# One tile's x in a full-array matmul and a one-bank buffer, and one batch's sums moved from TensorE to GpSimd

## The chip, the cores and the metric

The kernel runs on one core of one Trainium2 chip. The metric is the device time of the core in microseconds. Ratios here are the mean time of one kernel's fast runs over that of the other's of the same rounds, so they are not quite the ratio of the medians that stand beside them. The trace's span is about 1.8 us shorter than the device time.

## The reference, cut to what matters

```python
# attention with 32 memory slots, per batch and head (B=8, H=8, S=576, D=64, M=32)
a = exp(phi); a = a / a.sum(axis=sequence)          # "the sums": over the sequence
k_m, v_m = a.T @ k, a.T @ v                         # "the pooling"
attn = softmax(q @ k_m.T / 8)
x = attn @ v_m                                      # -> [B, S, 512]
# then a feed-forward block with layer norm and a residual
out = x + relu(layernorm(x) * g @ w_ch1) @ w_ch2    # 512 -> 2048 -> 512
```

Two batches are 1152 rows, which is nine tiles of 128. Tile 4 straddles the two batches; tile 8 is the ninth, and it lies in the second (odd) batch alone.

## The kernel before

Psum is where the matmuls of this kernel write. Tiles of a psum pool "big" have two banks each, three of them; those of "one" have one bank, two of them. `first layer` below means `mm1` (64 matmuls a batch), `second layer` means `mm2` (16 matmuls a tile, psum from "one").

```python
def a_exp(b):
    ...                                   # e = exp(phi) on ScalarE
    if b >= 2:                            # sums over the 9 chunks on GpSimd: six operations,
        ...                               # result split into two bf16 parts "hl"

def a_kv(b):
    ps = big([P, 2, 512], FP32, "kv_ps")
    a_sum(b, ps)                          # b < 2: nine matmuls; else two matmuls with hl
    a_pool(b, ps)                         # 72 matmuls in 64x32 tiles, then k, v and 1/sum out

def x_tiles(pr, ts, stats=True, o_ps=None):   # one or two tiles of x, row-tiled (64 rows each)
    if o_ps is None:
        o_ps = big([P, 2, 512], FP32, "o_ps")
    ...                                   # per tile: 4 matmuls, 8 where it straddles two batches
    x = moe.tile([P, 2, C], FP32, name="x_sb", bufs=4)
    nc.scalar.activation(out=x..., in_=o_ps..., func=AF.Copy)

# for batches b = 1..7; nb = b + 1; the odd ones finish five tiles, t = 4..8
half(0)                                   # first 8 matmuls of the second layer of t[0]
if more and odd:
    o_ps = big(...); kv_ps = big(...)
    a_sum(nb, kv_ps)
    x_tiles(pr, t[0:2], False, o_ps)
    a_pool(nb, kv_ps)
else:
    if more:
        a_kv(nb)
    x_tiles(pr, t[0:2], False)
x_tiles(pr, t[2:4], False)
if odd:
    x_tiles(pr, t[4:5], False)            # the ninth tile: fourth user of three "big" buffers
...
half(1)
```

The softmax here doesn't subtract the row's maximum and nothing guards it: scores larger than these inputs give would overflow.

## Time and profile before

| | before |
|---|---|
| device time, median of the first 3 runs | 250.44 us (250.23 to 250.91) |
| TensorE matmul busy | 95% of the span |
| chain that ended last | TensorE 77%, transfers 17% |
| first transposes of batch 1's q, second half | 47.1 us |
| first layer of batch 1 starts | 53.8 us |

The chain of waits is the view to read: up to 45 us it is transfers, after that TensorE to the end. The prediction shows its lines. Batch 7 in the chain in order of time (start, length, what), where there is no pooling left to do:

```profile
226.95 1.67 PE ch_ps L481 x7
228.62 0.79 PE o_ps L442 x24
229.41 3.99 PE ch_ps L481 x18
```

and GpSimd's first load for batch 4 in the timeline, which follows directly on the last of batch 3's sums:

```profile
80.72 0.43 POOL L201 TENSOR_TENSOR hl<-es,hl 128x128 bf16<-128x128 f32 x1
81.21 0.79 POOL L84 DMA_DIRECT2D kv_bf<-in_k_dram  x1
```

### The profile page before, as it was taken

Reading aid. Unit: us, or ns where it says so; the run is one execution under the profiler, and the core shown is the slowest. Engines: PE = TensorE matmul, PEld = TensorE weight load, DVE = VectorE, ACT = ScalarE, POOL = GpSimd, SP = SyncE. Lnnn points to the kernel's source line nnn. Section 1 sums busy time; section 2 is a strip of 40 time slices with the busy share of each in tenths; the row PEclk is TensorE's granted clock in tenths of the full one; section 3 lists DMA queues with packets and bytes.
Section 4 is the critical chain, followed back from the end, with each engine's and each line's share of the span. In section 5 each row is a group of like instructions: output and inputs, shape, how many; then the busy total and the mean of one; then the engine's idle time right before and its main releaser. Section 6 shows DMA issues by size and latency. Waiting matters only on the chain.

```text
span 248.8 us, 5860 instructions
## 1 busy us (share of the span) xinstructions
PE 236.5 (95%) x2460; PEld 132.2 (53%) x2491; DVE 156.0 (63%) x304; ACT 130.0 (52%) x219; POOL 60.7 (24%) x100
## 2 busy tenths in 40 slices
PE   7979899999999999999999999999999999999994
PEld 2544554457544665467544674466544764476442
DVE  3247663685577656687569637685679538783641
ACT  3164572587554465837472656655580755465310
POOL 8643241022325402090206202170205001000000
PEclk9999999999999999999999999999999999999999
DMA  7999999998499799919965997429983301203133
GB/s 150 190 202 206 207 256 213 286 223 148 119 174 236 116 216 245 179 20 194 262 122 117 146 242 168 104 37 221 211 167 68 73 14 43 45 12 75 42 84 84
DMA packets 42451, 36.82 MB, mean 148 GB/s; under 512 B 17461, under 2 KB 37689, under 8 KB 42425
## 3 DMA queue, kind: packets, MB, share of 16 engines
q0 software_dynamic: 17776, 19.53, 46.9%
q1 hardware_dynamic: 24488, 16.79, 28.4%
q8 instruction: 19, 0.31, 0.5%
q10 hardware_dynamic: 160, 0.13, 0.2%
q14 instruction: 8, 0.06, 0.1%
HBM read 41.42 MB, written 9.44 MB: 204 GB/s over the span
## 4 chain that ended last, share of the span: by engine, by line
PE 77%; DMA 17%; issue 2%; ACT 2%; POOL 1%; DVE 0%; POOLq 0%
PE ch_ps L481 45%; PE h_ps L411 22%; DMA q_bf<-in_q_dram 8%; DMA w1r<-in_moe_w_ch_dram 6%; DMA kv_bf<-in_k_dram 3%; PE w1b_ps L390 3%; PE o_ps L442 2%; PE last_ps L493 1%; ACT x_sb L448 1%; PE sc_ps L328 1%; PE den_ps L359 1%; PE kv_ps L210 1%; POOL q_bf L92 1%; PE qT_ps L310 0%; ACT qT L313 0%
## 5 line engine op out<-in xcount | busy, mean ns | idle before, releaser
L481 PE MATMUL ch_ps<-w2b,rT 128*128 128x512 bf16 x531 | 123.0, 379 | 2.3 <-issue 1.6
L481 PEld LDWEIGHTS <-rT 128*128 128x128 bf16 x560 | 52.1, 98 | 63.5 <-issue 6.5
L411 PE MATMUL h_ps<-Eh,w1b 128*128 128x288 bf16 x512 | 66.4, 285 | 1.3 <-ACT rT L417 1.0
L417 ACT ACTIVATE rT<-h_ps 128x576 bf16<-128x576 f32 x88 | 52.2, 648 | 26.8 <-PE h_ps L411 26.8
L411 PEld LDWEIGHTS <-w1b 128*128 128x128 bf16 x512 | 49.5, 97 | 18.1 <-issue 2.4
L394 DVE SCALAR_TENSOR_TENSOR w1b<-m_sb,rsum,w1b_ps 128x512 bf16<-128x512 f32 (+1 forms) x66 | 44.2, 726 | 8.5 <-PE w1b_ps L390 6.1
L419 DVE TENSOR_SCALAR rT<-h_ps 128x576 bf16<-128x576 f32 x40 | 30.3, 758 | 25.2 <-PE h_ps L411 24.6
L505 DVE SCALAR_TENSOR_TENSOR x_sb<-ch_ps,rstd,x_sb 128x512 f32<-128x512 f32 x35 | 26.1, 745 | 9.5 <-PE ch_ps L481 6.4
L461 DVE BATCH_NORM_STATS2 bst<-x_sb 128x6 f32<-128x512 f32 x36 | 24.3, 676 | 6.4 <-ACT x_sb L448 6.4
L448 ACT ACTIVATE x_sb<-o_ps 128x1024 f32<-128x1024 f32 (+1 forms) x20 | 17.8, 939 | 16.1 <-PE o_ps L442 16.0
L287 POOL TENSOR_TENSOR vb<-v,vmask 128x256 bf16<-128x256 bf16 x12 | 7.8, 664 | 60.9 <-DVE rs L237 60.9
L194 POOL TENSOR_TENSOR es<-e_sb 128x512 f32<-128x512 bf16 x6 | 6.9, 1156 | 62.2 <-ACT e_sb L187 62.2
L467 ACT ACTIVATE rstd<-mv,eps_sb 128x2 f32<-128x2 f32 (+1 forms) x20 | 5.9, 297 | 30.8 <-DVE mv L462 30.6
L333 ACT ACTIVATE E_sb<-sc_ps,rs 128x640 bf16<-128x640 f32 x16 | 11.8, 790 | 12.8 <-PE sc_ps L328 12.8
L375 DVE SCALAR_TENSOR_TENSOR Eh<-E_sb,rs,rden 128x576 bf16<-128x576 bf16 x16 | 12.4, 814 | 8.8 <-ACT rden L374 8.8
L179 PE MATMUL w_ps<-fill 128*128 128x512 f32 (+1 forms) x16 | 10.5, 774 | 1.6 <-DVE fill L119 1.6
L227 DVE CAST k<-kv_ps 128x256 bf16<-128x256 f32 x7 | 3.0, 425 | 13.8 <-PE kv_ps L210 13.8
L390 PE MATMUL w1b_ps<-w1r,kvT 64*32 64x512 bf16 (+1 forms) x264 | 10.9, 374 | 0.1
L187 ACT ACTIVATE e_sb<-phi_st 128x1152 bf16<-128x1152 f32 x8 | 9.2, 1151 | 2.7 <-DMA phi_st<-in_phi_dram 2.7
L374 ACT ACTIVATE rden<-rden 128x576 f32<-128x576 f32 x16 | 10.0, 672 | 0.1
L92 POOL DMA_DIRECT2D q_bf<-in_q_dram x10 | 7.6, 757 | 4.6 <-DMA w2b<-in_moe_w_ch_dram 1.8
L210 PE MATMUL kv_ps<-kv_bf,e_sb 64*32 64x128 bf16 (+1 forms) x648 | 7.4, 215 | 0.7 <-DMA kv_bf<-in_v_dram 0.4
(76 smaller groups left out, 150.9 us busy)
## 6 DMA issues: line engine op xcount, KB each, us to landing
out_dram<-x_sb SPq DMA_DIRECT2D x70, 128.0 KB, 2.9
kv_bf<-in_k_dram POOLq DMA_DIRECT2D x7, 576.0 KB, 6.1
kv_bf<-in_v_dram POOLq DMA_DIRECT2D x7, 576.0 KB, 9.5
phi_st<-in_phi_dram SPq DMA_DIRECT2D x6, 576.0 KB, 4.9
q_bf<-in_q_dram POOLq DMA_DIRECT2D x6, 576.0 KB, 13.6
w2b<-in_moe_w_ch_dram POOLq DMA_DIRECT2D x4, 512.0 KB, 17.8
w1r<-in_moe_w_ch_dram POOLq DMA_DIRECT2D x3, 512.0 KB, 14.2
q_bf<-in_q_dram POOLq DMA_DIRECT2D x4, 288.0 KB, 12.6
```

The costliest lines, as they stand in the source:

```text
L179: nc.tensor.matmul(w_ps[:, 0:N], fill[:, 0:P], fill[:, 0:N], start=True, stop=True)
L333: nc.scalar.activation(out=E_[:, g].rearrange("p (a x) -> p a x", a=2), in_=sc[:, :, 0:HP], func=AF.Exp, scale=s["rs"][:, g:g + 1])
L375: nc.vector.scalar_tensor_tensor(out=Eh[:, g, :], in0=s["E"][:, g, 0:S], scalar=s["rs"][:, g:g + 1], in1=rd[:, g].rearrange("p a x -> p (a ...
L390: nc.tensor.matmul(ps[32 * j:32 * (j + 1), g, 0:N], s["kvT"][r:r + 64, 2, 32 * j:32 * (j + 1)], w1r[r:r + 64, j, fs], start=True, stop=Tru ...
L394: nc.vector.scalar_tensor_tensor(out=s["w1b"][:, g, fs], in0=m_sb[:, fs], scalar=s["rsum"][:, g:g + 1], in1=ps[:, g, 0:N], op0=ALU.mult, o ...
L411: nc.tensor.matmul(h_ps[:, half, 0:HS], s["w1b"][:, g, P * j:P * (j + 1)], s["Eh"][:, g, HS * half:HS * (half + 1)], start=(g == 0), stop= ...
L417: nc.scalar.activation(out=dst, in_=h_ps[:, :, 0:HS], func=AF.Relu)
L419: nc.vector.tensor_scalar(out=dst, in0=h_ps[:, :, 0:HS], scalar1=0.0, scalar2=None, op0=ALU.max)
L448: nc.scalar.activation(out=x[:, 0:n].rearrange("p i (u y) -> p i u y", u=2), in_=o_ps.rearrange("p u (i y) -> p i u y", i=2)[:, 0:n], func ...
L461: nc.vector.bn_stats(out=stt, in_=x)
L481: nc.tensor.matmul(ch_ps, rT[:, j, P * t:P * (t + 1)], w2b[:, j, :], start=(j == 0), stop=(j == JC - 1))
L505: nc.vector.scalar_tensor_tensor(out=x, in0=ch_ps, scalar=rstd, in1=x, op0=ALU.mult, op1=ALU.add)
```

## The change

The ninth tile's x lies in one batch, so it can use the whole array: two matmuls with all 128 rows, into one bank of the small pool, rather than four with 64 rows into a large buffer. Its copy on ScalarE comes between those of the two pairs. The pooling comes ahead of all x, as in even batches. Apart from that, the sums of batch 1 move to GpSimd and behind that batch's pooling.

```diff
@@ a_exp
-        if b >= 2:
+        if b >= 1:
@@ a_kv, a_sum, a_pool
-        a_sum(b, ps)
-        a_pool(b, ps)
+        if b == 1:
+            a_pool(b, ps, lambda: a_sum(b, ps))     # called after the 72 matmuls
+        else:
+            a_sum(b, ps)
+            a_pool(b, ps)
     def a_sum(b, ps):
-        if b < 2:
+        if b < 1:
             kv_sum(b, ps)
@@ x_tiles: ahead of its copy
+        if mid is not None:
+            mid()
@@ new
+    def x_one(pr, t):
+        o_ps = one([P, C], FP32, "o1_ps")
+        ...
+        for g in range(2):
+            nc.tensor.matmul(
+                o_ps.rearrange("p (j e d) -> p j e d", e=2, d=D)[:, :, g, :],
+                s["Eh"][:, g, a:a + P], s["vb"][:, g].rearrange("p j d -> p (j d)"),
+                start=True, stop=True)
+        x = moe.tile([P, 2, C], FP32, name="x_sb", bufs=4)
+        nc.scalar.activation(out=x[:, 0], in_=o_ps, func=AF.Copy)
@@ batch loop
-        if more and odd:
-            ...                                     # first pair ahead of the pooling
-        else:
-            if more:
-                a_kv(nb)
-            x_tiles(pr, t[0:2], False)
-        x_tiles(pr, t[2:4], False)
-        if odd:
-            x_tiles(pr, t[4:5], False)
+        if more:
+            a_kv(nb)
+        x_tiles(pr, t[0:2], False)
+        x_tiles(pr, t[2:4], False, (lambda: x_one(pr, t[4])) if odd else None)
@@ start of batch 1
+    load(2)
     a_exp(1)
 ...
-    load(2)
     a_exp(2)
```

More of the change, by code (lines that the diff above doesn't have):

```diff
@@ L252, in a_sum, with a_pool @@
                                  start=(i == 0), stop=(i == 1))
-    def a_pool(b, ps):
+    def a_pool(b, ps, late_sum=None):
         kv_mm(b, ps, slice(0, 2))
+        if late_sum is not None:
+            late_sum()
         k_out(b, ps, b < 2)
@@ L422, with x_tiles @@
     xs = {}
-    def x_tiles(pr, ts, stats=True, o_ps=None):
+    def x_tiles(pr, ts, stats=True, mid=None):
         n = len(ts)
-        if o_ps is None:
-            o_ps = big([P, 2, 512], FP32, "o_ps")
+        o_ps = big([P, 2, 512], FP32, "o_ps")
         for i, t in enumerate(ts):
@@ L456, in x_tiles @@
                 x_stats(pr, t)
+    def x_one(pr, t):
+        o_ps = one([P, C], FP32, "o1_ps")
+        b = 2 * pr + P * t // S
+        a = P * t % S
+        s = st8[b]
+        for g in range(2):
[5 more added lines that the diff above has]
+        nc.scalar.activation(out=x[:, 0], in_=o_ps, func=AF.Copy)
+        mv = moe.tile([P, 2, 2], FP32, name="mv", bufs=4)
+        xs[(pr, t)] = (x[:, 0, :], mv, 0, 1)
     def x_stats(pr, t):
@@ L618 @@
         half(0)
-        if more and odd:
-            o_ps = big([P, 2, 512], FP32, "o_ps")
-            kv_ps = big([P, 2, 512], FP32, "kv_ps")
-            a_sum(nb, kv_ps)
-            x_tiles(pr, t[0:2], False, o_ps)
-            a_pool(nb, kv_ps)
-        else:
-            if more:
-                a_kv(nb)
-            x_tiles(pr, t[0:2], False)
-        x_tiles(pr, t[2:4], False)
-        if odd:
-            x_tiles(pr, t[4:5], False)
+        if more:
+            a_kv(nb)
+        x_tiles(pr, t[0:2], False)
+        x_tiles(pr, t[2:4], False, (lambda: x_one(pr, t[4])) if odd else None)
         if nb + 1 < B:
```

## The prediction

> **What bounds the kernel now.** I read four views: the busy shares, the chain of waits that ended last, the chain in order of time, and the timeline around the places that the change touches.
>
> The shares and the head of the chain first:
>
> ```profile
> PE 236.5 (95%) x2460; PEld 132.2 (53%) x2491; DVE 156.0 (63%) x304; ACT 130.0 (52%) x219; POOL 60.7 (24%) x100
> ...
> PE 77%; DMA 17%; issue 2%; ACT 2%; POOL 1%; DVE 0%; POOLq 0%
> ```
>
> The second line is the one to use: 77% of the span hangs on TensorE, 17% on transfers, and only 2% (about 5 us) on ScalarE. The chain in order of time shows where each lies. All the DMA is before 45.2 us (k, then a part of w1, then q of batch 1); after that it is TensorE to the end. So TensorE time that goes after 45.2 us is gained in full, and TensorE time that goes before is waited away on the transfer.
>
> Now the place where the ninth tile's x is made, batches 1, 3 and 5 (batch 3 looks the same as batch 1):
>
> ```profile
> 62.30 1.67 PE ch_ps L481 x7
> 63.97 0.03 PE kv_ps L251 x2
> 64.00 0.47 PE o_ps L442 x12
> 64.47 0.02 issue
> 64.50 1.03 ACT x_sb L448
> 65.53 0.04 issue
> 65.57 0.29 PE o_ps L442 x4
> 65.86 0.16 issue
> 66.02 1.67 PE ch_ps L481 x7
> ```
>
> Columns: start, length, what. Tempting reading: TensorE waits 1.03 us for a copy. The timeline corrects it:
>
> ```profile
> 64.38 0.80 PE L210 MATMUL kv_ps<-kv_bf,e_sb 64*32 64x128 bf16 x72
> 64.50 2.57 ACT L448 ACTIVATE x_sb<-o_ps 128x1024 f32<-128x1024 f32 x3 [2.03 <-PE o_ps L442]
> 65.12 0.74 PE L442 MATMUL o_ps<-vb,Eh 64*128 64x128 bf16 x12
> 65.57 0.11 PEld L442 LDWEIGHTS <-Eh 64*128 64x128 bf16 x3 [0.18 <-issue]
> ```
>
> During the copy TensorE does the 72 matmuls of the next batch's pooling and the second pair's x. Only the ninth tile's last group of four has to wait for the first pair's psum buffer (three large buffers: first pair, pooling, second pair; the ninth tile is the fourth user). The weight load before it sat idle for 0.18 us. So the wait is worth some 0.2 us a time, three times, not 1 us.
>
> From the last second-layer matmul's end to the next one's start it takes 66.02 - 63.97 = 2.05 us in batch 1, and 2.05 and 2.06 us in batches 3 and 5. The even batches, with pooling and four tiles, show the same stretch without a copy in it:
>
> ```profile
> 91.75 1.67 PE ch_ps L481 x7
> 93.43 0.03 PE kv_ps L251 x2
> 93.46 0.73 PE kv_ps L210 x72
> 94.19 0.55 PE o_ps L442 x16
> 94.74 0.16 issue
> 94.90 1.67 PE ch_ps L481 x7
> ```
>
> That is my yardstick: 0.034 us for each tiled x matmul, and 0.16 us of nothing when TensorE goes from tiled to full matmuls.
>
> Last, the sums of batch 1:
>
> ```profile
> 42.37 0.37 PE L218 MATMUL kv_ps<-ones,e_sb 128*128 128x2 bf16 x9
> 42.95 0.66 PEld L210 LDWEIGHTS <-e_sb 64*32 64x32 bf16 x72 [0.30 <-DMA kv_bf<-in_v_dram]
> 42.95 0.80 PE L210 MATMUL kv_ps<-kv_bf,e_sb 64*32 64x128 bf16 x72 [0.22 <-DMA kv_bf<-in_v_dram]
> ...
> 45.19 0.56 PEld L310 LDWEIGHTS <-q_bf 128*128 128x128 bf16 x10 [0.48 <-DMA q_bf<-in_q_dram]
> ```
>
> The nine sum matmuls stand before a wait for v and, a little later, one for q. Both are ended by transfers.
>
> **What the Trainium skill says.** "TensorEngine Tiling (Array Packing)", Key Properties: a change of tiling mode drains TensorE. The trace agrees: 0.16 us of idle where tiled x matmuls give way to full ones. "PSUM — Partial Sum Buffer", rule 1 of the four PSUM rules: one matmul's output fits in one bank of 512 fp32. That is why a full-array version of one tile (512 values a partition) fits the small buffer, while the row-tiled one, which runs two row tiles at once, spreads over two banks. "TensorE: Matmul & The Clock Gate", Back-to-back issue gap: 262 cycles for N=256 at the warm clock, or 0.109 us as an estimate from that page; the first layer agrees in this trace: 64 matmuls of 288 columns in 7.96 us are 0.124 us each, hence 0.11 us at 256. "GPSIMD Engine Reference", section 3.1: some 2.6 cycles an element for a two-input add. At 512 elements and 1.2 GHz that is 1.11 us as an estimate; the trace has 1.156 us.
>
> **The change part by part.**
>
> Ninth tile, batches 1, 3, 5. Removed: four row-tiled matmuls (4 x 0.034 = 0.14 us) and the wait of about 0.2 us. Added: two full matmuls of 256 columns, 2 x 0.11 = 0.22 us. The drain of 0.16 us is only moved, from ahead of the second layer to ahead of the two. Moved: the pooling now comes ahead of all x, as it does in even batches. New stretch: sums 0.03, pooling 0.73, first pair 0.47 (12 matmuls, eight of them for the tile that straddles two batches), second pair 8 x 0.034 = 0.27, drain 0.16, ninth tile 0.22, together 1.88 us against 2.05. Gain 0.17 us a time. Taking the x of b=7, whose 24 tiled matmuls last 0.79 us, as measure, the two pairs cost 0.79 - 0.14 = 0.65 us and the sum is 1.79: gain 0.26. I take 0.2, times three: 0.6 us.
>
> Ninth tile, batch 7. No pooling there and no buffer wait before: 24 matmuls in 0.79 us straight into the second layer. After: 0.65 + 0.22 plus perhaps a drain of 0.16, so 0.87 to 1.03. Loss 0.1 to 0.25, taken as 0.15 us.
>
> Buffers: the ninth tile takes the second of the two small psum buffers. I looked at which wait the next second-layer tile then carries: it is on ScalarE (the ninth tile's copy), not on the output of the tile before, so it takes the same buffer. The copy comes second on ScalarE (1.02 for the first pair, 0.60 for it), and ends about 1.7 us after the first pair is ready, while that tile starts some 2.7 us after. No stall. The copies and statistics come about 0.7 us later than before against an earlier TensorE, but the outputs that need them free a buffer only two tiles on, about 2.5 us of slack.
>
> Sums of batch 1. Removed: nine loads and matmuls, 42.16 to 42.74 us. All of it lies before the wait for v, so TensorE arrives earlier and waits longer: gain 0. Added on the path: two matmuls after the pooling, 0.03 us if the sums are there. Are they? The exponential starts at 38.60 and takes 1.15 us, to 39.75. GpSimd has issued its last load by 38.4. Batch 3's six operations ran from 77.28 to 81.15, 3.87 us; started 0.08 us after the exponential they end here at 43.70. The pooling ends at 42.95 + 0.73 = 43.68. That is a dead heat; with the wait's latency I expect the next second-layer matmul 0.05 to 0.3 us later than the 43.91 of now. Until q lands at 45.15 there are about 0.3 us of slack (0.30 us idle before the transposes), so most of it is swallowed. Cost taken as 0.1 us. The loads of batch 2 are moved in the text only: GpSimd's order has them in the same place, ahead of the new sums, with the same waits.
>
> Sum: -0.6 + 0.15 + 0.1 = -0.35 us.
>
> **The rivals.** (a) The whole 1.03 us of the copy in the chain is gained three times, 3.1 us less: about 247.3. Against it: the 72 pooling matmuls run within that time, and they must run somewhere. (b) GpSimd's sums come late, held by the shared port or slower than in batch 3 (the second one took 0.94 instead of 0.73 us beside a VectorE operation), and batch 1's kv evacuation, transposes and w1b all shift: 0.5 to 1 us more, about 251. For it: nothing after 45.2 us recovers lost time. Against it: VectorE runs one operation between 39.8 and 43.7, the output addition at 40.85. (c) The two full matmuls cost a second drain or an exposed weight load each: 0.2 us in four batches, so the gain is nil, 250.5. (d) An earlier TensorE in odd batches reaches a wait on the scores or on the first-layer weights sooner, and gives the gain back; the vector work for the next batch ends 6 us ahead of its use there, so I give it little.
>
> **Range and chances.** 250.44 - 0.35 = 250.09; I say 250.1. Range 249.4 to 250.8: the upper end holds (c) and half of (b), the lower a gain of 0.3 us a time with nothing lost elsewhere. The runs of before spread over 0.7 us by themselves. Two per cent would be 5 us, and no part of the change touches that much: same 0.98, faster 0.012, slower 0.008.
>
> **What would show it right or wrong.** In the changed profile: the stretch between second-layer matmuls in batches 1, 3, 5 at about 1.85 us, no ScalarE copy in the chain there; the stretch of batch 7 at 0.9 to 1.0 us; two x matmuls of 128 rows with about 0.11 us between them, after a single gap of 0.16; the first transposes of batch 1's q still at 45.2 us and still released by the transfer; GpSimd's sums ending at about 43.7 us. I am wrong if a wait for the sums on GpSimd stands in the chain, if the second-layer tile after the ninth tile's x waits on ScalarE, or if the q transfer itself lands at another time.

## The result, and the profile after

| | before | after |
|---|---|---|
| device time, median (4 runs each) | 250.61 us (250.23 to 250.91) | 250.62 us (250.24 to 250.69) |
| ratio, 95% interval | | 1.0 (0.9986 to 1.0014) |
| span of the profiled execution | 248.8 us | 248.8 us |

The spans agree to a tenth. The page's shares and chain for the changed kernel:

```profile
PE 239.4 (96%) x2476; PEld 132.2 (53%) x2476; DVE 156.5 (63%) x304; ACT 129.8 (52%) x219; POOL 64.2 (26%) x106
...
PE 79%; DMA 17%; POOL 1%; issue 1%; ACT 1%; DVE 0%; POOLq 0%
```

TensorE seems to do 2.9 us more work. It does not. The weight loads went from 2491 to 2476, which is right: nine sum matmuls fewer and two more, sixteen tiled x matmuls fewer and eight full ones more, in all 15 fewer. The matmuls went from 2460 to 2476 although they too are 15 fewer: the trace of the kernel before lacks 31 matmul records, this one lacks none. The changed kernel profiled again (e2) lacks 31 records too and reads 236.7 us, so the 2.9 us are the records. Busy time of a trace with missing records can't be compared, and it has a second effect, shown next.

The stretch around the x of batch 1, in the chain in order of time:

```profile
62.72 1.73 PE ch_ps L503 x8
64.44 0.03 PE kv_ps L254 x2
64.47 0.73 PE kv_ps L210 x72
65.20 0.68 PE o_ps L446 x20
65.88 0.33 PE o_ps L471 x2
66.21 1.73 PE ch_ps L503 x8
```

No copy in the chain, and TensorE goes without a break. Compare the groups of second-layer matmuls: `x8` in 1.73 us here, "0.16 issue" and then `x7` in 1.67 us in the kernel before. The eighth matmul of the group was run there too; its record is missing, and the gap is where it was. So the 0.16 us that I took for a drain was not all drain: where full matmuls follow full ones, the same missing record leaves a gap of 0.05 us (`62.24 0.05 issue` in the kernel before, then `x7` in 1.67 us). The rest is the drain. It is seen here as 1.83 instead of 1.73 us for eight matmuls after tiled ones (even batch, next fence), and as 0.33 us for two matmuls that stream in 0.22: 0.10 to 0.11 us.

So ends, not starts, must be compared. From the end of half(0) to the end of half(1): before 67.69 - 63.97 = 3.72 us, after 67.93 - 64.44 = 3.49 us. That is 0.23 us gained, in each of batches 1, 3 and 5. (67.69 and 67.93 are the starts of the transposes that follow in each chain.)

Batch 7 loses, as foreseen:

```profile
226.84 1.73 PE ch_ps L503 x8
228.57 0.68 PE o_ps L446 x20
229.25 0.32 PE o_ps L471 x2
229.57 12.09 PE ch_ps L503 x56
```

1.00 us of x instead of 0.79, but 0.10 of the difference is the drain that the next group pays in the kernel before. From batch 7's first layer to the start of the last matmuls it is 22.77 instead of 22.66 us: 0.11 lost.

Three times 0.23 less 0.11 is a gain of 0.6 us. Where did it go? Two places. The first is an even batch, number 2:

```profile
93.67 0.03 PE kv_ps L254 x2
93.70 0.73 PE kv_ps L210 x72
94.43 0.55 PE o_ps L446 x16
94.98 1.83 PE ch_ps L503 x8
...
96.98 1.73 PE ch_ps L503 x8
98.71 0.10 issue
98.81 0.47 PE sc_ps L333 x16
```

TensorE stops for 0.10 us ahead of the scores of batch 3 and then does them in 0.47 us rather than 0.40. In the kernel before there was no such stop.

The second is the opening. Timeline of the changed kernel:

```profile
43.29 0.43 POOL L201 TENSOR_TENSOR hl<-es,hl 128x128 bf16<-128x128 f32 x1
43.32 0.80 PE L210 MATMUL kv_ps<-kv_bf,e_sb 64*32 64x128 bf16 x72 [0.75 <-DMA kv_bf<-in_v_dram]
44.05 0.20 PE L254 MATMUL kv_ps<-ones,hl 128*128 128x2 bf16 x2
...
45.38 0.56 PEld L315 LDWEIGHTS <-q_bf 128*128 128x128 bf16 x10 [0.23 <-DMA q_bf<-in_q_dram]
...
47.58 0.56 PEld L315 LDWEIGHTS <-q_bf 128*128 128x128 bf16 x10 [0.65 <-DMA q_bf<-in_q_dram]
```

GpSimd's sums end at 43.72 us, and their two matmuls start at 44.05, straight behind the pooling: no wait. But v came at 43.3 and not 42.95 us, and the second half of q at 47.5 and not 47.1 us, and batch 1's first layer started at 54.28 and not 53.81 us. That 0.47 us, with the 0.18 us in batch 2, eats the gain. The question for the experiments is whether either belongs to the change.

For the steps from here on I use one table: starts of the first layer of batches 1 to 7 and of the last matmuls, read from the chain in order of time. The first column is when batch 1 starts; "tail" is from there to the start of the last matmuls; "1 to 2" is counted from the group after batch 1's first wait, which is 1.3 us after the start in all of them. Where nothing stops TensorE these steps repeat to 0.03 us between traces of the same code, while times of whole runs scatter by 0.5 us and more: the kernel before, over its 43 runs, went from 249.84 to 252.98 us, mean 250.79.

| trace | batch 1 | tail | 1 to 2 | 2 to 3 | 3 to 4 | 4 to 5 | 5 to 6 | 6 to 7 | 7 to last |
|---|---|---|---|---|---|---|---|---|---|
| before | 53.81 | 187.79 | 28.63 | 25.43 | 29.46 | 25.43 | 29.45 | 25.43 | 22.66 |
| after | 54.28 | 187.38 | 28.40 | 25.61 | 29.22 | 25.43 | 29.22 | 25.43 | 22.77 |
| e1 before again | 54.86 | 187.80 | 28.63 | 25.43 | 29.46 | 25.43 | 29.46 | 25.42 | 22.67 |
| e2 after again | 54.13 | 187.49 | 28.40 | 25.71 | 29.22 | 25.43 | 29.23 | 25.43 | 22.77 |
| e3 ninth tile only | 55.28 | 187.21 | 28.41 | 25.43 | 29.22 | 25.43 | 29.23 | 25.43 | 22.77 |
| e4 sums only | 54.20 | 187.99 | 28.63 | 25.62 | 29.46 | 25.43 | 29.45 | 25.43 | 22.67 |
| e5 order only | 54.68 | 187.69 | 28.60 | 25.42 | 29.43 | 25.43 | 29.42 | 25.42 | 22.67 |
| e6 ninth tile, b7 tiled | 54.24 | 187.26 | 28.40 | 25.59 | 29.22 | 25.43 | 29.22 | 25.43 | 22.67 |
| e7 sums slowed | 56.98 | 187.23 | 28.40 | 25.46 | 29.22 | 25.43 | 29.22 | 25.42 | 22.78 |
| e9 transpose early | 54.00 | 187.20 | 28.40 | 25.43 | 29.23 | 25.43 | 29.22 | 25.42 | 22.78 |
| e10 best | 53.77 | 187.10 | 28.40 | 25.43 | 29.23 | 25.43 | 29.22 | 25.42 | 22.67 |

(e8 and e11 are not in it: their chain leaves TensorE within batch 1 to 2; their tails are 187.45 and 187.94.)

### The profile page after: what moved, and what is told of

It reads as the page before. It is cut to its first block, busy times and chain, and to the rows that moved or that the text cites. A ratio compares the mean times of both kernels' runs of the same rounds, so it can differ in the third digit from the quotient of the medians.

```text
span 248.8 us, 5868 instructions
## 1 busy us (share of the span) xinstructions
PE 239.4 (96%) x2476; PEld 132.2 (53%) x2476; DVE 156.5 (63%) x304; ACT 129.8 (52%) x219; POOL 64.2 (26%) x106
## 4 chain that ended last, share of the span: by engine, by line
PE 79%; DMA 17%; POOL 1%; issue 1%; ACT 1%; DVE 0%; POOLq 0%
PE ch_ps L503 45%; PE h_ps L416 22%; DMA q_bf<-in_q_dram 8%; DMA w2b<-in_moe_w_ch_dram 6%; DMA kv_bf<-in_v_dram 4%; PE w1b_ps L395 3%; PE kv_ps L210 2%; PE o_ps L446 2%; PE last_ps L515 1%; PE sc_ps L333 1%; PE den_ps L364 1%; POOL q_bf L92 1%; PE o_ps L471 1%; POOL kv_bf L84 1%; ACT qT L318 0%
## 5 line engine op out<-in xcount | busy, mean ns | idle before, releaser
L503 PE MATMUL ch_ps<-w2b,rT 128*128 128x512 bf16 x560 | 128.3, 379 | 0.0
L527 DVE SCALAR_TENSOR_TENSOR x_sb<-ch_ps,rstd,x_sb 128x512 f32<-128x512 f32 x35 | 26.1, 746 | 9.7 <-PE ch_ps L503 7.8
L454 ACT ACTIVATE x_sb<-o_ps 128x1024 f32<-128x1024 f32 x16 | 16.0, 1026 | 18.2 <-PE o_ps L446 18.2
L194 POOL TENSOR_TENSOR es<-e_sb 128x512 f32<-128x512 bf16 x7 | 8.1, 1154 | 59.2 <-ACT e_sb L187 59.2
```

The costliest lines, as they stand in the source:

```text
L454: nc.scalar.activation(out=x[:, 0:n].rearrange("p i (u y) -> p i u y", u=2), in_=o_ps.rearrange("p u (i y) -> p i u y", i=2)[:, 0:n], func ...
L503: nc.tensor.matmul(ch_ps, rT[:, j, P * t:P * (t + 1)], w2b[:, j, :], start=(j == 0), stop=(j == JC - 1))
L527: nc.vector.scalar_tensor_tensor(out=x, in0=ch_ps, scalar=rstd, in1=x, op0=ALU.mult, op1=ALU.add)
```

## The experiments

**Theory A**: the change gains some 0.5 us after the opening, and the opening's 0.47 us is chance. **Theory B**: the sums on GpSimd, or the moved load, delay the opening.

### e1 and e2: both kernels again

No edit.

> The kernel before, unchanged, for the spread of its transfers and of its time. Theory A (the change gains some 0.5 us after 45 us, and the one profile of it had its q land 0.4 us later by chance): ratio 1.000 within 0.001, and the first transposes of q's second half start anywhere between 46.9 and 47.8 us; from the first h_ps matmul after the wait at about 55 us to the end it takes 193.7 us whatever the start. Theory B (the change itself delays the transfers): here the second half of q's transposes stay near 47.1 us.

> The changed kernel, unchanged. Theory A: q's second half again lands somewhere between 46.9 and 47.8 us, with no tie to the change; the part after the batch 1 start is 193.2 us; the ratio over many rounds falls to 0.998 (0.5 us of 250). Theory B: q's second half lands late again, at 47.5 us or more, and the ratio is 1.000.

| | median | ratio, 95% interval | batch 1 starts | tail |
|---|---|---|---|---|
| e1 before again | 250.76 us | 1.0008 (0.9975 to 1.0041) | 54.86 | 187.80 |
| e2 after again | 250.28 us | 0.9983 (0.9949 to 1.0017) | 54.13 | 187.49 |

The kernel before started batch 1 a full 1.05 us later than in its own first trace, and later than either trace of the changed kernel. In e2 q's second half was taken up at 47.2 us, where theory B expected 47.5 or more. So the opening scatters by more than the 0.47 us in question, whatever the kernel, and theory B has lost its reason; an effect smaller than this scatter is not excluded. In one of the traces the granted clock offers a cause. Columns of the windows view: stretch, its length, busy time and count of TensorE, weight loads, VectorE, ScalarE, GpSimd, then granted clock, transfers' share, GB/s. The kernel before, first trace, and after it e1:

```profile
16.00:20.00 4.00, 3.50 (x34) 1.97 (x34) 3.26 (x8) 2.74 (x6) 1.50 (x2) 1.00 1.27 205
```

```profile
16.00:20.00 4.00, 3.00 (x19) 1.61 (x18) 1.80 (x6) 2.57 (x5) 1.50 (x2) 0.65 1.28 204
```

Here TensorE ran at 0.65 of its clock for four microseconds of the opening and did 19 matmuls where it did 34; transfers moved the same. That it is the cause is not shown: in the same stretch e2 had a clock of 0.63 and e6 of 0.57, and they started batch 1 at 54.13 and 54.24 us, while e5 had 1.00 and started at 54.68. In the changed kernel's first trace the clock was 1.00, and there it was the transfers that came 0.3 us later: GpSimd issued the second half of q at 28.74 us, 28.41 in the kernel before, at a point where both programs had run the same instructions.

e2 also shows the dead heat between the sums and the pooling, this time lost. The sums on GpSimd started 0.6 us later here (40.49 us, 39.86 in the changed kernel's first trace). The granted clock was 0.63 from 16 to 20 us in this trace too, which may be why; that is argued, not shown:

```profile
43.93 0.43 POOL L201 TENSOR_TENSOR hl<-es,hl 128x128 bf16<-128x128 f32 x1
43.98 0.18 PE L254 MATMUL kv_ps<-ones,hl 128*128 128x2 bf16 x1
44.41 0.18 PE L254 MATMUL kv_ps<-ones,hl 128*128 128x2 bf16 x1 [0.25 <-POOL hl L201]
```

### e3 and e4: each part alone

e3 is the changed kernel with the sums of batch 1 as before; e4 is the kernel before with only the sums moved.

```diff
# e3, against the changed kernel (and load(2) back to its place)
-        if b >= 1:        # a_exp
+        if b >= 2:
-        if b < 1:         # a_sum
+        if b < 2:
-        if b == 1:        # a_kv: sums first again in every batch
-            a_pool(b, ps, lambda: a_sum(b, ps))
# e4, against the kernel before: the same lines the other way round
```

> Only the ninth tile's part; the sums of batch 1 on TensorE as before. Theory A: 193.2 us from batch 1's first layer to the end, ratio 0.998. Theory B (the sums on GpSimd delay the start): ratio 0.998 here too but 1.000 for the whole change, q landing near 47.1 us.

> Only the sums of batch 1 on GpSimd, after the pooling; the ninth tile as before. Theory A: ratio 1.000, the nine matmuls lay before a wait for v; 193.7 us from batch 1's first layer to the end. Theory B: ratio 1.001 to 1.002, the start of batch 1's first layer 0.4 us later than in the kernel before.

| | median | ratio, 95% interval | tail | step 2 to 3 |
|---|---|---|---|---|
| e3 ninth tile only | 250.30 us | 0.9988 (0.9953 to 1.0023) | 187.21 | 25.43 |
| e4 sums only | 251.20 us | 1.0028 (0.9990 to 1.0065) | 187.99 | 25.62 |

The steps add up. The ninth tile alone takes 0.58 us off the tail (three times 0.23, less 0.11) and leaves batch 2 alone. The sums alone add 0.20 us, all of it in batch 2, some 55 us after the sums were made. My expectation for e4's tail, the same as before, was wrong. Both times are inconclusive.

### e5: the order alone

```diff
# against the kernel before
-        if more and odd:
-            ...                                # first pair, then pooling
-        else:
-            if more:
-                a_kv(nb)
-            x_tiles(pr, t[0:2], False)
+        if more:
+            a_kv(nb)
+        x_tiles(pr, t[0:2], False)
```

> Only the order of the change: the pooling ahead of all x, and the ninth tile still row-tiled, in the large buffers. If the small buffer is what makes the order affordable: the ninth tile's four matmuls now wait for the first pair's copy, which starts only when the pooling and the first pair are done; the stretch from the end of one second-layer half to the end of the next grows from 3.7 to about 4.4 us in batches 1, 3, 5, a loss of 0.7 us a time or 2 us, ratio 1.008. If the order itself is what gains: ratio below 1.

Measured: median 250.72 us, ratio 0.9991 (0.9952 to 1.0030), tail 187.69 us. Expected was a loss of 2 us; there is none, and a gain of 0.03 us a time. The timeline:

```profile
65.53 1.17 PE L442 MATMUL o_ps<-vb,Eh 64*64 64x128 bf16 x24
...
66.09 2.43 ACT L448 ACTIVATE x_sb<-o_ps 128x1024 f32<-128x1024 f32 x3 [2.76 <-PE o_ps L442]
...
66.40 0.12 PEld L442 LDWEIGHTS <-Eh 64*128 64x128 bf16 x4 [0.30 <-DVE rs L237]
```

With the pooling first, the large buffer that comes free first is the pooling's, emptied by VectorE's three short operations, and not the first pair's, which ScalarE still copies. The pool gives the ninth tile that one. It waits 0.30 us for the reciprocal, not 0.7 us for the copy. So the order without the small buffer gains next to nothing: of the 0.23 us, 0.20 is the small buffer with its full matmuls.

### e6: the ninth tile of batch 7 as before

```diff
# against e3
-        x_tiles(pr, t[2:4], False, (lambda: x_one(pr, t[4])) if odd else None)
+        x_tiles(pr, t[2:4], False, (lambda: x_one(pr, t[4])) if odd and more else None)
+        if odd and last:
+            x_tiles(pr, t[4:5], False)
```

> Candidate for the best: only the ninth tile's part, and in batch 7, where nothing had to wait, the ninth tile row-tiled as before; sums of batch 1 on TensorE. From batch 1's first first-layer matmul to the end of the last one of the kernel: 191.46 us in the kernel before, 3 x 0.23 less is 190.77, and 0.1 less than with the ninth tile of batch 7 as full matmuls. Ratio 0.997. If the full matmuls cost nothing in batch 7, 190.9 as with the ninth tile's part alone.

Measured: median 250.23 us, ratio 0.9985 (0.9938 to 1.0031); batch 7 takes 22.67 us again, 0.10 less than with full matmuls. The tail was 187.26 and not 187.1 us, because batch 2 took 25.59 us here, with no sums on GpSimd at all. So those sums are not what the stop in batch 2 needs.

### e7: the sums slowed

```diff
# against the changed kernel
-            nc.gpsimd.tensor_tensor(out=a4, in0=ev[:, 0:4], in1=ev[:, 4:8], op=ALU.add)
+            for _ in range(3 if b == 1 else 1):
+                nc.gpsimd.tensor_tensor(out=a4, in0=ev[:, 0:4], in1=ev[:, 4:8], op=ALU.add)
```

> The changed kernel with GpSimd's first add of batch 1 done three times: the sums end 2.4 us later, about 46.2 us. If the sums are at the edge of the path, TensorE waits for them after the pooling for some 2 us, and the first layer of batch 1 starts 1.5 to 2 us later than with the sums as changed: ratio 1.006 to 1.008. If the wait for q hides them: 1.000.

Measured: median 253.73 us, ratio 1.0111 (1.0071 to 1.0151). Batch 1 starts at 56.98 us, 2.7 us later than in the changed kernel's first trace.

```profile
45.18 0.29 POOL L201 CAST hl<-es 128x128 bf16<-128x128 f32 x1
45.52 0.10 PEld L255 LDWEIGHTS <-hl 128*128 128x128 bf16 x1 [2.08 <-POOL hl L201]
...
46.03 0.18 PE L255 MATMUL kv_ps<-ones,hl 128*128 128x2 bf16 x1 [0.32 <-POOL hl L202]
```

TensorE waits 1.95 and then 0.32 us for GpSimd, and nothing later gives it back: the wait for q is used up. The loss is larger than expected. So the sums stand right at the edge of the path: 2.4 us of delay cost all of it, and as changed they have no slack to speak of.

### e8: six tiny fills in the place of the six operations

```diff
# against e3 (with load(2) ahead of a_exp(1), as in the changed kernel)
+    padt = consts.tile([P, 2], FP32, name="padt")
     load(2)
+    for _ in range(6):
+        nc.gpsimd.memset(padt, 0.0)
     a_exp(1)
```

> Only the ninth tile's part, with six tiny fills on GpSimd in the place where the six operations of batch 1's sums stand. All three profiles with those sums show a wait of 0.43 us ahead of GpSimd's load of batch 4's k, and a step from batch 2's first layer to batch 3's of 25.61 us; none of the three without them does (25.43). If it is the number of GpSimd's instructions that does it: the wait and 25.61 here too. If it is what those operations do or what waits on them: no wait, and 25.43.

Measured: median 250.35 us, ratio 0.9973 (0.9936 to 1.0011). GpSimd's load of batch 4's k in the timeline, the changed kernel first, then e8:

```profile
80.95 0.43 POOL L201 TENSOR_TENSOR hl<-es,hl 128x128 bf16<-128x128 f32 x1
81.81 0.79 POOL L84 DMA_DIRECT2D kv_bf<-in_k_dram  x1 [0.43 <-issue]
```

```profile
80.15 0.43 POOL L201 TENSOR_TENSOR hl<-es,hl 128x128 bf16<-128x128 f32 x1
81.00 0.79 POOL L84 DMA_DIRECT2D kv_bf<-in_k_dram  x1 [0.43 <-issue]
```

The wait of 0.43 us is there with six fills that feed nothing. All six traces with just six more GpSimd instructions (after, e2, e4, e8, e9, e11) have it; none of those with no more (before, e1, e3, e5, e6, e10) has it, nor e7 with eight more. It goes with where the instruction stands in GpSimd's stream. Why is not shown, but the kept traces hold a hint: of the queue that the page calls "instruction", q14, all six have one packet in the DMA view between 79 and 86 us, and none of the other seven has any. So GpSimd may have waited for its next instructions to be fetched.

The step from 1 to 3 took 54.08 us here, 0.24 more than e3's 53.84. And here the chain itself runs through the stop, and names it:

```profile
84.38 13.57 DMA qT<-q_bf
97.95 0.14 issue
98.08 0.47 PE sc_ps L330 x16
```

The scores of batch 3 wait for the transpose of q by DMA, which landed 13.6 us after its issue. In the kernel before it took 13.2 us and landed at 84.94 + 13.2 = 98.1 us, 0.26 us ahead of the scores at 98.40. Less than half of that is slack. In the seven traces in which the scores are held up (after, e2, e4, e6, e7, e8, e11) they start 0.14 us after the landing, in those in which they are not and the transpose has its old place (before, e1, e3, e5) 0.24 to 0.27 us after it. So there was some 0.12 us of slack, and what the transpose takes beyond it is the stop: 0.30 us longer gives 0.18 us (after), 0.85 us longer gives 0.73 us (e11, from batch 1 to 3). The chain of e2 names another releaser, a VectorE output (`98.01 0.76 DVE x_sb L527`). That is a coincidence: in the kernel before this output ends at 98.7 us, when the scores have already started.

The transposes of the traces without the stop took 13.2 us (before, e1, e3, e5) or 13.4 (e7, held up by 0.03 us), with it 13.5 to 14.1 us (after, e2, e4, e6, e8, e11). All five traces with GpSimd's late load and the transpose in its old place (after, e2, e4, e8, e11) belong to the second group; but e6, with no late load, does too. So the late load may lengthen the transpose, by coming into its time, and is not its only cause.

### e9: the transpose of batch 3's q issued earlier

In batch 1 it stands behind the outputs of tile 7 in the sync queue, and so waits for that tile's second layer, though its data landed 4 us earlier.

```diff
# against the changed kernel
-            mm2_out(pr, t[3])
             if b == 1:
                 a_qT(nb + 1, 0)
+            mm2_out(pr, t[3])
```

> The changed kernel, with the transpose of batch 3's q issued ahead of the outputs of the tile before instead of behind them. In the three profiles with batch 1's sums on GpSimd the step from batch 2's first layer to batch 3's is 25.61 us, not 25.43, and I put that down to this transpose landing 13.5 us after its issue, just too late for the scores. If so: the transpose lands about 95 us, the step is 25.43 again, and from batch 1's first layer to the start of the last matmuls it takes 187.2 us, not 187.4 to 187.5. If the delay has another cause, the step stays at 25.61.

Measured: median 250.37 us, ratio 0.9994 (0.9970 to 1.0018). The transpose is issued at 80.2 us and lands 10.0 us later, the step from batch 2 to 3 is 25.43 us, and the tail 187.20 us, although GpSimd's late load is there (0.41 us). The starts in the chain:

```profile
83.69 7.96 PE h_ps L416 x64
109.12 7.96 PE h_ps L416 x64
138.35 7.96 PE h_ps L416 x64
```

That settles the stop in batch 2: it is the transpose's landing, and an earlier issue takes it away. The time of this call's runs does not show it; three of the six had a mean clock of 0.993 or less over the whole run, and where in the run is not on record.

### e10: the parts that gain, together

e6 and the early transpose.

> Candidate for the best: the ninth tile as full matmuls in batches 1, 3 and 5 only, sums of batch 1 on TensorE, the transpose of batch 3's q issued early. From batch 1's first layer to the start of the last matmuls 187.80 - 3 x 0.235 = 187.1 us, with steps of 29.70, 25.43, 29.22, 25.43, 29.22, 25.43 and 22.67. Ratio 0.997, which the scatter of the opening may hide.

Measured: median 250.37 us, before 250.80 us in the same rounds, ratio 0.9981 (0.9964 to 0.9998), tail 187.10 us with every step as expected. It is the only version here whose interval lies below 1, and by 0.0002; among eleven runs that would be weak evidence alone, and it is the steps that carry it. The gain is 0.2%.

### e11: batch 1's sums ahead of its pooling

```diff
# against the changed kernel
-        if b == 1:
-            a_pool(b, ps, lambda: a_sum(b, ps))
-        else:
-            a_sum(b, ps)
-            a_pool(b, ps)
+        a_sum(b, ps)
+        a_pool(b, ps)
```

> The changed kernel with batch 1's sums ahead of its pooling, as in all later batches. GpSimd's sums end at 43.7 us and the pooling's v lands at 43.0 to 43.3: TensorE now waits for GpSimd 0.4 to 0.7 us longer, and the pooling ends as much later, at 44.5 instead of 44.0. Of that the wait for q's second half swallows most: the first layer of batch 1 starts 0 to 0.5 us later, ratio 0.998 to 1.001.

Measured: median 251.45 us, ratio 1.0015 (0.9991 to 1.0039). TensorE waits 0.71 and 0.33 us for the two parts of the sums, the pooling starts at 44.36 us, and batch 1's first layer at 54.78 us, 0.5 us later than in the changed kernel's first trace. The tail of 187.94 us has the longest of the transposes in it, 14.1 us. So where GpSimd makes these sums, the place behind the pooling is the better one; it hides about 0.7 us of the wait. The wait is in the trace; that the later start comes from it is argued, as the opening scatters by as much.

## Why the prediction was right or wrong

The time was right: 250.1 predicted, 250.62 measured, inside 249.4 to 250.8, and no difference over 2% as forecast. The ten runs of the changed kernel have a mean of 250.42 us, the 43 runs of the kernel before 250.79: the difference of 0.37 us is close to the 0.35 predicted, but it is smaller than the scatter of single runs and shown by the steps of the traces, not by the times. That the sum came out is partly luck. By the steps 0.70 us were gained in batches 1, 3 and 5, 0.11 lost in batch 7 and 0.18 to 0.28 in batch 2. The last was not foreseen; it fell where the prediction had a gain 0.1 us too small and 0.1 us set aside for the opening.

- **What bounds it, and the rival of 1.03 us a time**: right. The copy left the chain and 0.23 us a time came back (28.63 to 28.40, 29.46 to 29.22 us), because the pooling ran under the copy.
- **Gain of 0.2 us a time, 0.6 in all**: right in sum (0.23 and 0.7), but terms were mis-read. Of the "0.16 us of nothing" taken for a drain some 0.05 us is the missing record of one matmul; the drain is 0.10 us (1.83 less 1.73). A tiled x matmul takes 0.028 us and not 0.034 (in batch 7, 24 took 0.79 us before and 20 take 0.68 now: 0.11 for four). So four tiled matmuls gave way to two full ones that cost 0.11 us more, and what the wait and the old order cost was, as an estimate, 0.23 + 0.11 = 0.34 us rather than 0.2.
- **Loss in batch 7, 0.15 us**: 0.11 measured, just the dearer matmuls. Part of a drain was counted in the 0.15, but the drain is paid in the kernel before too.
- **The next second-layer tile takes the ninth tile's small buffer and doesn't wait**: right; no ScalarE copy in the changed chain. That the order alone would cost 0.7 us a time (e5's expectation) was wrong: another large buffer comes free first.
- **Sums of batch 1: nine matmuls gained nothing, a dead heat with the pooling, 0.1 us**: the dead heat is right, to 43.72 against 44.05 us in one trace and 0.25 us of wait in another. e7 shows how near it is. Whether 0.1 us is lost in the opening can't be told: batch 1 starts anywhere from 53.48 us (e8) to 55.28 us (e3) in traces without the sums on GpSimd, from 54.00 to 54.28 in those with them behind the pooling and not slowed.
- **"An earlier TensorE in odd batches reaches a wait on the scores ... so I give it little"**: this is the step that failed. There was such a wait, in batch 2, an even one where I had not looked, with some 0.12 us to spare, and it took back 0.18 to 0.28 us of the 0.6. I looked at VectorE's work for the next batch and not at the transpose by DMA that the same scores need. It was not TensorE's earlier arrival that used up the slack: the transpose is issued 1.20 us after batch 2's first layer starts in both kernels, so it moves along, and e3 kept the slack. It was a transpose 0.3 us longer. Why it took longer stays open.
- **"The loads of batch 2 are moved in the text only"**: right for those loads. That six more GpSimd instructions would hold up a load of batch 4 by 0.43 us was not foreseen.
- **q at another time** was named as what would make me wrong. It landed 0.4 us later in the changed trace, before which the programs had not differed. In e1 batch 1 of the unchanged kernel starts later still, although q's second half landed at 46.7 us there, earlier than the 47.1 of its first trace: the opening hangs on more than q.

## What to carry to other kernels

A copy in the chain of waits is worth only the idle time of the bound engine under it, not its length: look up what that engine does meanwhile. When two traces differ by less than runs scatter, compare steps between fixed points of the chain; they repeat to 0.03 us here where whole runs differ by 0.5 us and more, and they say which batch lost. And list every input of a stage before calling it slack: the vector work was 6 us early, the transpose of the same stage about an eighth of a microsecond.

## What the Trainium skill lacked or had wrong

- "TensorEngine Tiling (Array Packing)", Key Properties: it says that a change of tiling mode drains TensorE, without a figure. These traces show 0.10 us when tiled matmuls give way to full ones (eight second-layer matmuls in 1.83 us after x tiles, 1.73 us otherwise), and about as much the other way: 24 w1b matmuls took 0.77 us behind full ones, and three times the 0.22 us of eight that follow tiled ones is 0.66.
- "GPSIMD Engine Reference", section 3.1: 2.6 cycles an element fit the 512-element add (1.11 us worked out from it, 1.156 measured), but smaller operations took longer than that rate gives, and the section has no figure for it: 256 elements took 0.763 us on average (0.55 by the rate, an estimate), 128 took 0.43 to 0.46 us (0.28 by the rate), a cast of 128 0.291 us.
- No page has it: a pause of 0.43 us ahead of a GpSimd transfer issue that came and went with the number of GpSimd instructions before it (in every trace with six more, whatever these did; in none with none more or with eight more). A packet of the "instruction" queue q14 falls near it in these six traces alone; the cause is open.
- "DMA: Bandwidth & Descriptors", DMA Transpose (X-bar): it gives the path and its limits, but no time from issue to landing within a queue of other transfers. The transpose of one batch's q took 13.2 to 14.1 us while the loads of the next batch ran, and 10.0 and 10.3 us when issued almost 5 us earlier (80.2 instead of 85.2 us).
- "Perfetto Trace Analysis", section "Tensor Engine Instruction (MATMUL, LD_WEIGHTS)", says that TensorE's end times are a model. It does not say that records can be missing: 31 of 2491 matmuls in the kernel before, none of 2476 in the changed kernel's first trace and 31 in its second, and the gap that one leaves reads as idle time (0.05 us between full matmuls) or swells a real one (0.16 us for a drain of 0.10).
